# Theta and the token products take their token tiles in the order in which the MLP finishes them

## The chip, the cores and the metric

The kernel runs on one core of a Trainium2 chip. The metric is the device time of one execution in microseconds; the time of a kernel is the median of several runs. The engines are TensorE (PE, matmuls; PEld is its weight load), VectorE (DVE), ScalarE (ACT), GpSimd (POOL) and SyncE (SP), which issues most of the DMAs. Each engine works through its own instructions in one fixed order and waits for the others by semaphores.

## What is computed

The program is a chain of three blocks on 2 batches of 768 tokens: bucketed attention (8 heads of 64), a block that adds the real part of a 2D Fourier transform and then an MLP (512 to 2048 to 512), and a last block. The change lies in the last block:

```python
def _moe2_ref(x, w_theta, w_tok_r, w_tok_i, w_ch):
    theta = x @ w_theta
    cos_t, sin_t = (np.cos(theta), np.sin(theta))
    zr = x * cos_t
    zi = x * sin_t
    yr = np.einsum('ts,bsd->btd', w_tok_r, zr)
    yi = np.einsum('ts,bsd->btd', w_tok_i, zi)
    y = yr + yi
    u = x + y
    return (u + np.maximum(u @ w_ch, 0.0)).astype(np.float32)
```

Its x is the MLP block's result. The token products (yr, yi) sum over all 768 source tokens s, so the order in which the source tiles are added is free.

## The kernel before, in words

Tokens are held in 6 tiles of 128 (NT = 6). Most products are made of three matmuls (P3): high by high, high by low, low by high, where each operand is split into a rounded high part and a rest.

**The MLP** (`mlp1`, `mlp2`, from line 799 for the second) works on groups of two tiles. Group g holds tiles g and g + 3, so the groups finish tiles 0 and 3, then 1 and 4, then 2 and 5. This is also the list `order` of line 716, [0, 3, 1, 4, 2, 5], which the layer norm uses. At the end of each group two DVE operations add the sums, which lie in two PSUM banks, to the residual u of the two tiles.

**theta** (line 821) then goes tile by tile over u. For each tile PE transposes it in four pieces (`psf<-ident,u` in the trace); ACT rounds the transposed tile to xh, DVE makes the rest xl; ACT makes a copy xs, which SP writes to DRAM (`xT<-xs`); PE makes 12 products with the theta weights (`psf<-wthh,xh` and the like). Then come the argument reduction, sine and cosine on ACT (nn<-psf first), POOL and DVE (rr<-nn,psf first), and the four parts of z (zr and zi, high and low) for the tile. The buffers xh, xl and xs exist once, nn and rr twice.

**tok_sum** (line 862) makes one half (384 of the 768 target tokens) of the token product of one batch: for each of 4 blocks kd of 128 channels, 6 source tiles of 6 matmuls, 144 in all. With `s_outer` the source tiles are the outer loop and four banks are summed at once, so that the sum can follow theta. Otherwise each block kd is summed on its own. **conv_tok** (line 1025) converts the token weights of a half, two pieces for each source tile (real and imaginary, n = 2s + r), in the order n = 0 to 11: a DMA brings them (`r<-in_wtok`), two ACT operations and one DVE operation decode them, ACT writes the high part (w1h; wtx for source tile 5) and POOL the low part. The second half's pieces are written over those of the first half.

**The order of the work.** Outside attention nothing is ordered by hand: a planner places the instructions of each engine by their data dependences and by priorities that `at` and `timed` give (a start and a step in us), on a timeline of its own. Around the change the program's order is: theta of batch 0, the MLP of batch 1 (groups 0, 1, and `mlp1` of group 2), the first half's token weights, `mlp2` of group 2 (line 1034), theta of batch 1 (line 1055), tok_sum of batch 0, half 0 (line 1058), tok_sum of batch 1, half 0, with `s_outer` (line 1068), the second half's weights (line 1070), the channel product of batch 0 half 0, then the second halves. Sums named psm in the trace use three PSUM banks (the MLP and most token sums); those named psf use five (theta, and the sum with `s_outer`).

Most instructions are issued through one helper, so the line in the trace is L62 for nearly all of them; the names of the tiles tell them apart.

Of the kernel before, what the change touches and what calls it, by code (L numbers as in the profile page):

```python
# [22 lines left out]
NT = S // 128  # L23
# [10 lines left out]
def f(t):  # L34
    return t.bitcast(F32)
# [35 lines left out]
def fused_kernel(ctx, tc, A, out):  # L71
# [9 lines left out]
    def mm(o, l, r, st, sp):  # L81
        PE.matmul(o, l, r, start=st, stop=sp)
# [4 lines left out]
    def stt(eng, out, in0, in1, op, scale=1.0):  # L87
        if eng is V:
            return V.scalar_tensor_tensor(out=out, in0=in0, scalar=scale, in1=in1, op0=ALU.mult, op1=op)
        assert scale == 1.0  # L90
        return eng.tensor_tensor(out=out, in0=in0, in1=in1, op=op)
# [34 lines left out]
    def PS1():  # L126
        return PS(now[0])
# [588 lines left out]
    order = [g + 3 * i for g in range(3) for i in range(2)]  # L716
# [101 lines left out]
    z_t = {}  # L818
    xTd = {b: mk(dr_p, [128, 4, S], F32, f"xT{b}") for b in range(B)}

    def theta(b, wth, zt):
        x2 = u_t[b]
        for t in range(NT):
            c = slice(128 * t, 128 * t + 128)
            pt = PS1()
            for kd in range(4):
                PE.transpose(pt[:, 128 * kd:128 * kd + 128], x2[:, t, 128 * kd:128 * kd + 128], ident)
            xh = zt([128, 4, 128], F32R, "xh")
            xl = zt([128, 4, 128], F32R, "xl")
            pk = pt.rearrange("p (k n) -> p k n", k=4)  # L830
            AC.activation(out=xh, in_=pk, func=AF.Copy)
            V.tensor_tensor(out=xl, in0=pk, in1=f(xh), op=ALU.subtract)
            xs = zt([128, 4, 128], F32, "xs")
            AC.activation(out=xs, in_=pt.rearrange("p (k n) -> p k n", k=4), func=AF.Copy)
            SY.dma_start(out=xTd[b][:, :, c], in_=xs)
            xx = (xh, xl)
            th = PS1()
            n = 0
            for kd in range(4):
                for a, k in P3:  # L840
                    mm(th, xx[a][:, kd], wth[k][:, kd], n == 0, n == 11)
                    n += 1
            nn = zt([128, DM], F32, "nn")
            AC.activation(out=nn, in_=th, func=AF.Identity, scale=1.0 / TWO_PI, bias=c_mag)
            PL.tensor_scalar(out=nn, in0=nn, scalar1=1.0, scalar2=-MAGIC, op0=ALU.mult, op1=ALU.add)
            rr = zt([128, DM], F32, "rr")
            V.scalar_tensor_tensor(out=rr, in0=nn, scalar=-PC1, in1=th, op0=ALU.mult, op1=ALU.add)
            V.scalar_tensor_tensor(out=rr, in0=nn, scalar=-PC2, in1=rr, op0=ALU.mult, op1=ALU.add)
            PL.tensor_scalar(out=rr, in0=rr, scalar1=3.1415925, scalar2=-3.1415925, op0=ALU.min, op1=ALU.max)
            V.tensor_scalar(out=nn.bitcast(U32), in0=rr.bitcast(U32), scalar1=0x7FFFFFFF, scalar2=None, op0=ALU.bitwise_and)  # L850
            AC.activation(out=rr, in_=rr, func=AF.Sin)
            AC.activation(out=nn, in_=nn, func=AF.Sin, scale=-1.0, bias=c_pi2)
            for r, trig in enumerate((nn, rr)):
                stt(V if r else PL, trig, trig, x2[:, t], ALU.mult)
                zh, zl = z_t[b][r]
                AC.activation(out=zh[:, t], in_=trig, func=AF.Copy)
                stt(PL if r else V, zl[:, t], trig, f(zh[:, t]), ALU.subtract)
            yield

    TH = 384  # L860

    def tok_sum(b, half, wt, kx, s_outer=False):

        c = slice(TH * half, TH * half + TH)
        xt, uh, ul = kx
        SY.dma_start(out=xt, in_=xTd[b][:, :, c])

        def sums(ps, kd, s):
            n = 0
            for r in range(2):  # L870
                for a, k in P3:
                    mm(ps[:, 0:TH], z_t[b][r][a][:, s, 128 * kd:128 * kd + 128], wt(k, r, s), s == 0 and n == 0, s == NT - 1 and n == 5)
                    n += 1

        def split(ps, kd):
            V.tensor_tensor(out=xt[:, kd], in0=ps[:, 0:TH], in1=xt[:, kd], op=ALU.add)
            AC.activation(out=uh[:, kd], in_=xt[:, kd], func=AF.Copy)
            V.tensor_tensor(out=ul[:, kd], in0=xt[:, kd], in1=f(uh[:, kd]), op=ALU.subtract)

        if s_outer:  # L880
            pss = [PS1() for _ in range(4)]
            for s in range(NT):
                for kd in range(4):
                    sums(pss[kd], kd, s)
                yield
            for kd in range(4):
                split(pss[kd], kd)
            return
        for kd in range(4):
            ps = PS1()  # L890
            for s in range(NT):
                sums(ps, kd, s)
            split(ps, kd)
            yield
# [109 lines left out]
    def zt(shape, dt, tag):  # L1004
        n = turn.get(tag, 0)
        turn[tag] = n + 1
        return mk(zts[n % len(zts) if tag in ("nn", "rr") else 0], shape, dt, tag)
# [3 lines left out]
    zz = lambda p, tag: mk(p, [128, NT, DM], F32R, tag)  # L1011
    z_t[0] = [[zz(x_p, "x"), zz(zb_p, "za")], [zz(zb_p, "zb"), zz(zb_p, "zc")]]
    timed(theta(0, wth, zt), T["z0"], 2)
    now[0] = "m"
    mlp(1, T["m1"], range(2))
# [5 lines left out]
    def wt(k, r, s):  # L1021
        n = 2 * s + r
        return w1z[k][:, TH * n:TH * n + TH] if n < 10 else wtx[0][:, 2 * k + n - 10]
# [29 lines left out]
    timed(conv_tok(0, 10), t0 - 14, 1)  # L1053
    now[0] = "f"
    timed(theta(1, wth, zt), t0 - T["tp"], 1)
    now[0] = "m"
    k0 = operands(xt_p, xt_p)
    timed(tok_sum(0, 0, wt, k0), t0 + 20, 2)
    zt2_p.release()
    zt_p.release()  # L1060
# [5 lines left out]
    k1 = operands(xt1_p, u1_p)  # L1066
    now[0] = "f"
    timed(tok_sum(1, 0, wt, k1, True), t0 + 40, 2)
    now[0] = "m"
    timed(conv_tok(1), t0 + 40, 1)  # L1070
    timed(tok_out(0, 0, wch, k0), t0 + 56, 1)
    k0 = operands(xt_p, xt_p)
    timed(tok_sum(1, 1, wt, k0), t0 + 60, 2)
    now[0] = "f"
    timed(tok_out(1, 0, wch, k1), t0 + 70, 1)
# [109 lines left out]
```

## Time and profile before

| | us |
|---|---|
| median of 3 runs | 728.55 |
| the runs | 728.55, 734.02, 728.23 |
| the profiled execution | 728.28 |
| its span, first to last instruction | 726.5 |
| PE busy in the span | 664.8 |
| DVE, ACT, POOL busy | 402.6, 372.7, 370.1 |

All rows below are from the one profiled execution, with times from the span's start. A share of busy time is an average over stages with different limits; the stages around theta and the token sums are read by themselves.

### The profile page before, as it was taken

The page shows a single profiled execution, that of the slowest core. Times are in us where ns is not written, and L with a number is a line of the kernel's source. Part 1 is how long each engine was busy: PE and PEld are TensorE (multiplying, and loading weights), DVE is VectorE, ACT ScalarE, POOL GpSimd, SP SyncE. Part 2 cuts the span into 40 slices and gives each one's busy share as a digit, 9 for nine tenths or more (in the row PEclk, how much of TensorE's full clock was granted, in tenths as well). Part 3 has the DMA queues.
Part 4 walks back from the last instruction along what each step waited for, and adds up shares of the span by engine and source line. Part 5 has one row for each costly group of instructions (what it writes and reads, how often), then busy time and mean ns, then how long its engine had stood idle before and what let it go on. Part 6 is the DMA issues. An engine that isn't in the chain of part 4 may idle for free.

```text
span 726.5 us, 13450 instructions
## 1 busy us (share of the span) xinstructions
PE 664.8 (92%) x5424; PEld 510.9 (70%) x5424; DVE 402.6 (55%) x655; ACT 372.7 (51%) x597; POOL 370.1 (51%) x312
## 2 busy tenths in 40 slices
PE   5798988669668898999999999999999899999998
PEld 2365556557557655786686786687485599999997
DVE  1566787865999665543377583255422476751222
ACT  2565565766988898773423152065325676730010
POOL 3787789586878888776660020033403446930000
PEclk9999999978699999999999999999999999999999
DMA  9896967459889999776560043011004631720202
GB/s 327 186 187 141 157 121 142 93 164 213 197 206 240 269 231 253 151 145 124 102 195 27 13 120 65 1 45 30 1 1 145 223 89 39 234 81 25 88 1 87
DMA packets 161469, 93.68 MB, mean 129 GB/s; under 512 B 137088, under 2 KB 147584, under 8 KB 161408
## 3 DMA queue, kind: packets, MB, share of 16 engines
q1 hardware_dynamic: 159472, 86.27, 51.3%
q0 software_dynamic: 1936, 6.57, 2.6%
q8 instruction: 42, 0.69, 0.4%
q14 instruction: 19, 0.16, 0.1%
HBM read 49.82 MB, written 6.29 MB: 77 GB/s over the span
## 4 chain that ended last, share of the span: by engine, by line
PE 48%; POOL 10%; issue 9%; DMA 6%; ACT 5%; DVE 4%; POOLq 0%; SPq 0%; DVEq 0%; ACTq 0%
PE psm L62 31%; PE psf L62 14%; POOL p L62 3%; ACT r L62 2%; PE pso L62 2%; POOL w1l L62 2%; DMA x<-p 2%; POOL stk L62 2%; PE pss L62 1%; DMA r<-in_wtok 1%; DMA r<-in_w 1%; POOL pt L62 1%; DVE r L62 1%; ACT stk L62 1%; POOL w2l L62 1%
## 5 line engine op out<-in xcount | busy, mean ns | idle before, releaser
L62 PE MATMUL psm<-unT,w1h 128*128 128x256 f16 x768 | 130.4, 274 | 0.1
L62 PE MATMUL psm<-unT,w1l 128*128 128x256 f16 x384 | 105.2, 274 | 0.0
L62 DVE SCALAR_TENSOR_TENSOR r<-r 128x512 uint32<-128x512 uint32 (+1 forms) x64 | 64.6, 1016 | 51.9 <-ACT r L62 49.2
L62 PEld LDWEIGHTS <-w1h 128*128 128x128 f16 (+1 forms) x774 | 75.1, 99 | 15.5 <-issue 4.5
L62 PEld LDWEIGHTS <-hh 128*128 128x128 f16 x384 | 37.1, 98 | 42.8 <-issue 2.2
L62 POOL TENSOR_TENSOR w1l<-r,w1h 128x384 fp32r<-128x384 f32 (+1 forms) x36 | 41.9, 1178 | 43.5 <-ACT w1h L62 43.5
L62 PE MATMUL pss<-stk 128*128 128x384 f32 x192 | 48.8, 384 | 15.2 <-ACT p L62 9.4
L64 PE MATMUL pss<-stk 64*128 64x384 f32 (+1 forms) x288 | 55.4, 470 | 6.4 <-ACT p L64 3.2
L62 DVE TENSOR_REDUCE nm<-pss 128x1 f32<-128x768 f32 x48 | 44.9, 949 | 29.0 <-PE pss L62 28.8
L62 PE MATMUL psm<-w2h,hl 128*128 128x512 f16 x192 | 60.3, 379 | 0.0
L62 PE MATMUL psm<-w2l,hh 128*128 128x512 f16 x192 | 59.8, 379 | 0.2 <-POOL w2l L62 0.2
L62 ACT ACTIVATE r<-r,chalf 128x512 uint32<-128x512 uint32 (+1 forms) x64 | 46.1, 720 | 26.2 <-DMA r<-in_wtok 10.2
L62 PE MATMUL psm<-w2h,hh 128*128 128x512 f16 x192 | 59.3, 379 | 0.0
L62 POOL TENSOR_TENSOR p<-p,p 128x768 f16<-128x768 f32 x32 | 54.7, 1715 | 6.6 <-ACT p L62 5.5
L62 ACT ACTIVATE p<-pss,nm 128x768 f32<-128x768 f32 x48 | 42.5, 892 | 28.1 <-DVE nm L62 23.3
L62 DVE SCALAR_TENSOR_TENSOR hl<-psm,hh 128x512 f16<-128x512 f32 x48 | 32.8, 687 | 41.9 <-ACT hh L62 41.8
L64 DVE TENSOR_REDUCE nm<-pss 128x1 f32<-128x768 f32 x48 | 43.6, 950 | 19.9 <-PE pss L64 19.8
L62 ACT ACTIVATE hh<-psm 128x512 f16<-128x512 f32 x48 | 28.2, 590 | 40.4 <-PE psm L62 40.4
L62 PEld LDWEIGHTS pss<-stk 128*128 128x128 f32 x192 | 34.6, 204 | 20.2 <-ACT p L62 11.9
L62 PEld LDWEIGHTS <-w1l 128*128 128x128 f16 x384 | 37.7, 98 | 5.7 <-issue 1.2
L62 ACT ACTIVATE r<-r 128x512 f32<-128x512 f32 (+1 forms) x64 | 39.5, 618 | 0.0
L62 POOL TENSOR_TENSOR stk<-tt,stk 64x768 fp32r<-64x768 f32 x16 | 31.1, 1945 | 11.5 <-issue 9.6
(322 smaller groups left out, 1552.2 us busy)
## 6 DMA issues: line engine op xcount, KB each, us to landing
r<-in_w SPq DMA_DIRECT2D x32, 512.0 KB, 4.5
r<-in_wtok SPq DMA_DIRECT2D x24, 384.0 KB, 3.8
vr<-in_v SPq DMA_DIRECT2D x8, 390.0 KB, 3.6
stk<-stk SPq DMA_DIRECT2D x16, 192.0 KB, 3.8
xT<-xs SPq DMA_DIRECT2D x12, 256.0 KB, 2.6
xt<-xT SPq DMA_DIRECT2D x4, 768.0 KB, 5.8
ct<-in_ct POOLq DMA_DIRECT2D x4, 579.0 KB, 7.3
sn<-in_sn POOLq DMA_DIRECT2D x4, 576.0 KB, 8.2
```

Source lines behind the costliest of these rows:

```text
L62: return fn(*a, **k)
L64: self.last = fn(*a, **k)
```

## The change

Theta and both forms of the token sum take the tiles in `order` instead of 0 to 5; the closing matmul of a sum is that of the last tile in `order`, which is tile 5 in both.

```diff
     def theta(b, wth, zt):
         x2 = u_t[b]
-        for t in range(NT):
+        for t in order:
             c = slice(128 * t, 128 * t + 128)
...
-                    mm(ps[:, 0:TH], z_t[b][r][a][:, s, 128 * kd:128 * kd + 128], wt(k, r, s), s == 0 and n == 0, s == NT - 1 and n == 5)
+                    mm(ps[:, 0:TH], z_t[b][r][a][:, s, 128 * kd:128 * kd + 128], wt(k, r, s), s == 0 and n == 0, s == order[-1] and n == 5)
...
         if s_outer:
             pss = [PS1() for _ in range(4)]
-            for s in range(NT):
+            for s in order:
                 for kd in range(4):
                     sums(pss[kd], kd, s)
...
             ps = PS1()
-            for s in range(NT):
+            for s in order:
                 sums(ps, kd, s)
```

Both batches use these functions. The order in which `conv_tok` makes the weights stays 0 to 5.

## Rows read from the trace of the kernel before

**Rows 1.** The page, part 1: busy us, share of span, instructions.
```profile
PE 664.8 (92%) x5424; PEld 510.9 (70%) x5424; DVE 402.6 (55%) x655; ACT 372.7 (51%) x597; POOL 370.1 (51%) x312
```

**Rows 2.** Busy time by stage: stretch, length, then engines, PEclk, DMA share, GB/s.
```profile
573.85:580.65 6.80, 4.58 (x28) 4.25 (x26) 2.92 (x6) 5.21 (x10) 2.87 (x3) 1.00 0.96 314
...
614.24:639.38 25.14, 25.14 (x146) 25.14 (x146) 18.28 (x19) 20.57 (x41) 23.62 (x19) 1.00 0.61 189
...
sum 242.96, PE 240.72 PEld 207.38 DVE 104.14 ACT 96.98 POOL 75.44; mean PE 40.12 PEld 34.56 DVE 17.36 ACT 16.16 POOL 12.57
```

**Rows 3.** Waits of PE, 480 to 727: us in total, times, longest.
```profile
PE psf L62 <- DVE u L62: 2.2, 1, 2.2
```

**Rows 4.** PE's timeline, 578 to 582: start, us, operation, idle before it.
```profile
578.09 0.34 PE L62 MATMUL psm<-w1l,x 128*128 128x384 f32 x1
580.65 0.66 PE L62 MATMUL psf<-ident,u 128*128 128x128 f32 x4 [2.22 <-DVE u L62]
581.06 0.42 PE L62 MATMUL psm<-w1h,za 128*128 128x384 f32 x1
...
581.84 0.34 PE L62 MATMUL psm<-w1h,x 128*128 128x384 f32 x1
```

**Rows 5.** DVE's timeline, 568 to 582.
```profile
568.82 0.69 DVE L62 TENSOR_TENSOR xl<-psf,xh 128x512 fp32r<-128x512 f32 x1 [0.43 <-ACT xh L62]
...
579.30 0.69 DVE L62 SCALAR_TENSOR_TENSOR rr<-nn,psf 128x512 f32<-128x512 f32 x1 [0.58 <-POOL nn L62]
579.91 1.28 DVE L62 SCALAR_TENSOR_TENSOR u<-psm,u 128x512 f32<-128x512 f32 x2
```

**Rows 6.** ACT's timeline, 568 to 630.
```profile
568.21 0.58 ACT L62 ACTIVATE xh<-psf 128x512 fp32r<-128x512 f32 x1
...
576.69 0.76 ACT L62 ACTIVATE r<-r,chalf 128x512 uint32<-128x512 uint32 x1 [1.37 <-DMA r<-in_wch]
...
577.89 0.67 ACT L62 ACTIVATE nn<-psf,cmag 128x512 f32<-128x512 f32 x1
...
629.20 0.98 ACT L62 ACTIVATE w1h<-r 128x384 fp32r<-128x384 f32 x2
```

**Rows 7.** DVE's timeline: the MLP's last additions, batch 0, and batch 1's second group.
```profile
359.25 1.29 DVE L62 SCALAR_TENSOR_TENSOR u<-psm,u 128x512 f32<-128x512 f32 x2
...
525.46 1.29 DVE L62 SCALAR_TENSOR_TENSOR u<-psm,u 128x512 f32<-128x512 f32 x2 [3.07 <-PE psm L62]
```

**Rows 8.** PE's timeline: theta's products of batch 1, second to fourth tile.
```profile
568.84 0.50 PE L62 MATMUL psf<-wthh,xh 128*128 128x512 f32 x1
...
571.95 0.60 PE L62 MATMUL psm<-w2h,hl 128*128 128x512 f16 x2
...
585.16 0.39 PE L62 MATMUL psf<-wthh,xh 128*128 128x512 f32 x1
...
592.96 0.39 PE L62 MATMUL psf<-wthh,xh 128*128 128x512 f32 x1
```

**Rows 9.** SP's timeline, 586 to 623: issues of DMAs.
```profile
586.71 21.90 SPq L62 DMA_DIRECT2D xT<-xs  x4
...
622.42 0.58 SPq L62 DMA_DIRECT2D xt<-xT  x1
```

**Rows 10.** POOL's timeline: low parts of the token weights, both halves.
```profile
570.76 1.03 POOL L62 TENSOR_TENSOR w1l<-r,w1h 128x384 fp32r<-128x384 f32 x1 [1.69 <-ACT w1h L62]
...
637.03 2.37 POOL L62 TENSOR_TENSOR w1l<-r,w1h 128x384 fp32r<-128x384 f32 x2 [0.41 <-ACT w1h L62]
641.36 2.52 POOL L62 TENSOR_TENSOR wtx<-r,wtx 128x384 fp32r<-128x384 f32 x2 [1.96 <-ACT wtx L62]
```

**Rows 11.** DVE's timeline: the last part of z, batch 1.
```profile
633.70 0.68 DVE L62 SCALAR_TENSOR_TENSOR za<-nn,u 128x512 fp32r<-128x512 f32 x1
```

**Rows 12.** PE's timeline: first products of z's last tile, first of the second half.
```profile
635.06 0.51 PE L62 MATMUL psf<-wtx,u 128*128 128x384 f32 x2
...
647.55 0.35 PE L62 MATMUL psm<-w1h,u 128*128 128x384 f32 x1
```

## The prediction

> **What bounds the kernel now.** I read the whole page first, then a table by stage, then the waits, then single instructions. The page has TensorE (PE) busy for 92% of the span and every other engine for near half [rows 1]. The table by stage then takes the second half: over six stretches from 480.00 us to the last matmul at 722.96, PE is busy for 240.72 of 242.96 us, and the loss of 2.2 us lies in one of them, 573.85 to 580.65, where it works 4.58 us of 6.80; the granted clock stays at 1.00 there [rows 2]. The list of PE's waits in that half has one entry: 2.2 us, once, for VectorE's (DVE) write of u [rows 3]. So behind 480 us the kernel is a queue of matmuls with one hole of 2.22 us, and no order of tiles can give back more than that hole there.
>
> PE's timeline shows what stands at the hole: token products of batch 0 run up to 578.09, and the next four of the same block (za, zb, zb, zc of the fifth token tile, from 581.06) are held, since ahead of them in PE's order stand the four transposes of theta's third tile of batch 1 (tile 2), which wait for u [rows 4]. Tile 2 is written with tile 5 by the two additions that end the third MLP group. DVE makes them only at 579.91: ahead in its queue is the theta reduction of the second tile (rr<-nn,psf), which waits for GpSimd (POOL) [rows 5]. POOL waits for ScalarE (ACT), whose rounding of that tile (nn<-psf) comes at 577.89, behind 1.37 us of waiting for a weight load (in_wch) and the decoding of what it brought [rows 6].
>
> **What the change removes.** In the new order theta's third and fourth tiles are 1 and 4. Both are written by the additions of the second MLP group at 525.46 [rows 7], some 45 us before they are wanted. Nothing then ties the third tile to the end of the third group. Tile 2 comes fifth; in before the fifth tile's transposes lie behind the fourth's first products at 592.96 [rows 8], over 11 us behind the additions. The wait goes, if PE has something else to run until 580.65, that is 6.80 us of work from 573.85 on. It has the 30 matmuls of the first block of token sums, at 25.14/144 = 0.175 us each [rows 2] 5.2 us; and the third tile's theta: four transposes, 0.41 us from 580.65 to the next matmul [rows 4], and 12 products, which for the second tile run from 568.84 to 571.95 with one MLP matmul among them [rows 8], about 2.9 us. Together 8.5 us against 6.8: enough by 1.7. Where a part of it runs before 573.85 it pushes the MLP's end back by as much, which costs PE nothing.
>
> **What it adds: no work.** The same instructions on other slices: six theta tiles for each batch, 144 matmuls for each token sum, the same DMAs and the same weights. For batch 0 all six tiles are there long before theta takes them (its MLP's last additions come at 359.25 [rows 7]): 0 us.
>
> **What it moves.** Three things, each costed at 0 with its cover:
> - Tile 2's copy to DRAM goes out fifth, not third, on SP's queue. The load of batch 1's first residual half needs tiles 0 to 2; in before it is issued at 622.42, behind all six copies [rows 9]. Cover: the sixth copy is out before it too.
> - The fifth token tile's weights are now wanted fourth. The last of them is converted at 571.79 [rows 10]; their sums start at about 577.9 (two of six run before the hole [rows 4]) and would start 6 x 0.175 = 1.05 us sooner. Cover: 5 us.
> - The second half's weights overwrite the first half's, in the order 0 to 5, while batch 1's sums now free these in the order 0, 3, 1, 4, 2, 5. The sums run 25.14 us [rows 2], 4.2 us a tile, so tile 1's place comes free 4.2 us later and tile 2's 8.4 us later, at 614.24 + 5 x 4.2 = 635.2; the weights of tiles 3 and 4 queue behind. Six low parts at 1.19 us on POOL from about 636 end at 643, the last two, 2.52 us together, at 645.7 [rows 10]. The first reader starts at 647.55 [rows 12], the last tile's 30 matmuls (5.2 us) later. Cover: 4 us for those wanted first, 7 for the last. If it were gone, each us late would be one of PE's, which has nothing else to run there.
>
> **What is late next.** With the hole closed, batch 1's sums start at 612.0 and want the last tile's z at 632.8. In before that z ends at 634.38 [rows 11], only 0.7 us ahead of its first matmul at 635.06 [rows 12]. But theta lost time at its third tile: these products start 16.3 us behind the second's (568.84, 585.16), the fourth's 7.8 us behind the third's [rows 8]. So theta should end some 8 us sooner, and this slack grows. Were theta to end where it did, 1.6 us of the gain would go (the bound above).
>
> **The sum.** The profiled execution took 728.28 us (span 726.5); less 2.22 it is 726.06. The median of the runs is 728.55, 0.27 above the profiled one, so the forecast is 726.3 us. What the trace can't show is the order in which the planner, with its own timeline, puts the new work on each engine. That is bounded by the rows: at best nothing beyond the 2.22, at worst the slower rivals below; I take 0, nearest to how theta's second tile fared, whose products came with no idle time.
>
> **The rivals.**
> (a) *The hole stays in another form.* The second block of token sums needs a PSUM bank, and the additions that write u also free the MLP's two banks: its first matmul starts at 581.84, right behind them [rows 4, 5]. If the third tile's operands aren't ready at 578.43, PE runs the four left-over matmuls (0.7 us) and waits for the same DVE operation: 728.55 - 0.7 = 727.9. For it: ACT is what was late in before. Against it: the third tile gives PE 3.3 us of other work. [...]
> (b) *Slower: theta jumps ahead on PE and waits for ACT.* The planner may now put the third tile's 12 products right behind the MLP. Their xh is ACT's work; if it stands where the second tile's nn stood, at 577.89, then xh (0.58) [rows 6] and xl (0.69) [rows 5] make the products start at about 579.2. PE would stand up to 579.2 - 573.85 = 5.35 us in place of 2.22: 731.7. It decides on how many token matmuls stand ahead of them: 30 hide it all, under 18 the kernel is slower than before. Against it: the second tile's products came 0.02 us behind the start of xl, with MLP matmuls in front and no idle.
> (c) *Slower: the second half's weights jam ACT.* If tile 2's conversion, held to 635.2 instead of its 629.20 [rows 6], stands in ACT's queue ahead of the last theta tile's work, that z comes 6 us late, at 640.4 against 632.8 wanted: 7.6 lost less 2.2, near 734. Against it: theta should be done with ACT by then.
>
> **How the numbers follow.** Forecast 0.60 (725.5 to 727.0: the full gap, give or take 0.7); (a) 0.22, with the case that the planner moves nothing and the time stays at 728.5; (b) 0.12; (c) 0.06. The range goes from 725.0 (the lowest run, 728.23, less the gap, less 1 for run and overlap) to 730.0, half of (b)'s price: it leaves out the worse half of (b) and (c), a little over a tenth. A measurement tells about 1% (7.3 us) from no change. The gain can't reach that by what stands above: faster 0.02. Slower by over 1% needs (c) with some of (b): 0.05. Within it: 0.93.
>
> **What would show it.** Right: no wait of PE for DVE's u behind 545 us and PE busy throughout behind the MLP's end; theta's third tile inside or right behind the third MLP group, its products under 10 us after the second's; tile 2's transposes fifth; batch 1's sums starting near 612. Wrong: a PE wait for xl or xh near 574 to 580 (b), for u with a token matmul at its head (a), for z or the second half's weights between 630 and 655 (c), or idle time of PE anywhere that was dense.

## The result, and the profile after

The changed kernel takes 735.11 us (median of 10 runs, 733.68 to 737.14). The kernel before, run beside it, took 730.5 us. The ratio is 1.0069, 95% interval [1.0046, 1.0091]: about 5 us slower, where 2.2 us less was forecast, and outside the range (725.0 to 730.0). The profiled execution took 733.68 us, with a span of 731.9.

One remark on the base. In later runs of the kernel before, the medians were 730.7 to 731.3 and single runs went from 726.9 to 735.8. So its profiled execution of 728.28 us is a low one of its spread. Ratios below are taken over the undisturbed runs and needn't equal the quotient of the medians over all runs; single profiles are used to see where time goes.

The page's first part and the list of PE's waits of the changed kernel (380 to 732 us: total, times, longest):

```profile
PE 664.9 (91%) x5424; PEld 509.9 (70%) x5424; DVE 403.7 (55%) x655; ACT 372.4 (51%) x597; POOL 371.2 (51%) x312
```
```profile
PE psm L62 <- DVE xt L62: 4.0, 1, 4.0
PE psf L62 <- ACT xh L62: 2.6, 2, 2.3
```

PE has the same 5424 matmuls and all but the same busy time [rows 1]. The one entry of before, for u [rows 3], is gone. In its place stand 2.6 us for ACT's xh and a new 4.0 us for DVE's xt.

**The front.** PE's timeline around the old hole (start, us, operation, idle before it and what ended it):

```profile
568.17 0.50 PE L62 MATMUL psf<-wthh,xh 128*128 128x512 f32 x1 [0.31 <-ACT xh L62]
...
568.74 0.27 PE L62 MATMUL psf<-ident,u 128*128 128x128 f32 x1
...
571.31 0.49 PE L62 MATMUL psf<-ident,u 128*128 128x128 f32 x3
...
573.14 0.59 PE L62 MATMUL psm<-w2h,hl 128*128 128x512 f16 x2
573.39 0.52 PE L62 MATMUL psm<-w1h,x 128*128 128x384 f32 x1
...
576.39 0.34 PE L62 MATMUL psm<-w1l,zb 128*128 128x384 f32 x1
579.03 0.50 PE L62 MATMUL psf<-wthh,xh 128*128 128x512 f32 x1 [2.30 <-ACT xh L62]
```

The third tile's four transposes (psf<-ident,u) run inside the MLP; its last two matmuls start at 573.14 and the token products of batch 0 follow, as forecast. But PE's order then has the third tile's products behind only 17 token matmuls (the first at 573.39, the last at 576.39), and these products wait 2.30 us. ACT's timeline says for what:

```profile
576.11 0.76 ACT L62 ACTIVATE r<-r,chalf 128x512 uint32<-128x512 uint32 x1 [1.35 <-DMA r<-in_wch]
...
577.31 0.68 ACT L62 ACTIVATE nn<-psf,cmag 128x512 f32<-128x512 f32 x1
...
578.40 0.59 ACT L62 ACTIVATE xh<-psf 128x512 fp32r<-128x512 f32 x1
```

It is the wait of before [rows 6]: ACT stands 1.35 us in front of a load of in_wch, the weights of the channel product, then decodes it, then does the second tile's nn and the third tile's xh. Before, this chain ran on over POOL and DVE to u; now it ends at xh. The hole is 2.30 us where it was 2.22.

**The back.** PE's timeline from the start of batch 1's sums to the second halves:

```profile
613.90 0.33 PE L62 MATMUL psf<-w1h,u 128*128 128x384 f32 x1
...
644.93 0.34 PE L62 MATMUL psm<-ks,wchl 128*128 128x384 f32 x1
649.24 0.74 PE L62 MATMUL psm<-ks,wchh 128*128 128x384 f32 x2 [3.96 <-DVE xt L62]
...
652.98 0.35 PE L62 MATMUL psm<-w1h,u 128*128 128x384 f32 x1
```

The stalled matmul belongs to the channel product of batch 0 half 0, which has four blocks of 12 matmuls and three PSUM banks. Its fourth block can start only when an eviction has freed the first block's bank. These evictions are DVE's `xt<-psm,xt`. DVE's and ACT's timelines:

```profile
644.75 0.56 DVE L62 SCALAR_TENSOR_TENSOR r<-r 128x384 uint32<-128x384 uint32 x1 [1.20 <-ACT r L62]
645.22 0.55 DVE L62 TENSOR_TENSOR u<-xt,u 128x384 fp32r<-128x384 f32 x1
645.69 0.55 DVE L62 TENSOR_TENSOR xt<-psf,xt 128x384 f32<-128x384 f32 x1
646.16 2.56 DVE L62 TENSOR_TENSOR u<-xt,u 128x384 fp32r<-128x384 f32 x2
648.64 1.47 DVE L62 SCALAR_TENSOR_TENSOR xt<-psm,xt 128x384 f32<-128x384 f32 x3
```
```profile
636.65 0.64 ACT L62 ACTIVATE r<-r,chalf 128x384 uint32<-128x384 uint32 x1 [3.62 <-DMA r<-in_wtok]
...
638.60 0.53 ACT L62 ACTIVATE w1h<-r 128x384 fp32r<-128x384 f32 x1
...
643.57 0.65 ACT L62 ACTIVATE r<-r,chalf 128x384 uint32<-128x384 uint32 x1 [1.71 <-DMA r<-in_wtok]
...
644.56 0.92 ACT L62 ACTIVATE u<-xt 128x384 fp32r<-128x384 f32 x2
```

Read from the bottom up. The evictions (648.64) stand behind the splits of batch 1's sum (u<-xt,u). The splits need ACT's copies u<-xt (644.56), which stand behind the decoding of a second-half weight; that stood 1.71 us waiting for its load. DVE's own decoding of that weight (644.75) is ahead of the splits as well. The two splits at 646.16 take 1.28 us each, where the one at 645.22 took 0.55; POOL makes low parts beside them (646.00 to 648.30), but that this slows them wasn't tested. In the kernel before two such splits took 2.22 us (642.07), so it is not new. The load is late for the reason that POOL and SP show:

```profile
639.21 1.04 POOL L62 TENSOR_TENSOR w1l<-r,w1h 128x384 fp32r<-128x384 f32 x1 [3.44 <-ACT w1h L62]
```
```profile
624.18 16.42 SPq L62 DMA_DIRECT2D r<-in_wtok  x6
...
640.28 0.33 SPq L62 DMA_DIRECT2D r<-in_wtok  x1
```

The raw weights land in a small ring of buffers r. A buffer comes free when POOL has made the low part from it, and POOL can write that only over a place that the sums have left. The sums now leave tile 2's place fifth, while its pieces still come third in the converting order; these hold their buffers, and the last load goes out at 640.28, just as POOL's low part of 639.21 ends (640.25). POOL had waited 3.44 us for ACT's high part of that piece (638.60). Tile 2's place was free at 634.70, where the sums' last tile begins, but ACT stood 3.62 us, until 636.65, in front of another late load: here one late load made the next one late. The rows don't name the piece; that it is tile 2's is argued from the order, and the first experiment tests it. In the kernel before the same six issues, and the first evictions, stood so (SP, then DVE):

```profile
624.31 9.41 SPq L62 DMA_DIRECT2D r<-in_wtok  x6
```
```profile
644.22 1.01 DVE L62 SCALAR_TENSOR_TENSOR xt<-psm,xt 128x384 f32<-128x384 f32 x2
```

There the last issue was over at 633.72, and the first eviction ended near 644.7, only 0.7 us before its bank was wanted (12 matmuls, 2.1 us, ahead of 647.55 [rows 12], so 645.4).

**The clock.** Busy time by stretch of the changed kernel (columns as [rows 2]):

```profile
645.00:649.20 4.20, 0.27 (x2) 0.00 (x0) 4.20 (x7) 1.80 (x5) 2.30 (x2) 1.00 0.00 0
649.24:651.00 1.76, 1.76 (x6) 1.76 (x7) 0.87 (x2) 0.00 (x0) 0.00 (x0) 0.60 0.22 81
651.00:653.00 2.00, 2.00 (x8) 2.00 (x8) 0.00 (x0) 0.00 (x0) 0.00 (x0) 0.50 0.34 125
653.00:660.00 7.00, 7.00 (x42) 7.00 (x41) 0.56 (x1) 0.00 (x0) 0.00 (x0) 1.00 0.43 149
```

Behind the gap PEclk, TensorE's granted clock, is 0.60 in the mean and then 0.50, until about 653; from there it is 1.00. The 12 matmuls of the fourth block take 3.74 us (649.24 to 652.98); at 0.175 each it would be 2.10, so 1.64 us more.

**The account.** From the last two matmuls of batch 1's MLP to the kernel's last matmul, the kernel before needs 149.35 us (573.26 to 722.61) and the changed one 154.91 (573.14 to 728.05): 5.56 more. The parts: 0.08 (2.30 for 2.22), 3.96 for the bank and 1.64 at the lower clock, together 5.68. Against this, the changed kernel ran four transposes ahead of this stretch that the kernel before has in it, 0.41 us [rows 4]; for equal work the difference is 5.97, of which 0.3 us has no row here. This stretch is called the tail below; each tail is that of one execution.

### The profile page after: what moved, and what is told of

Read it like the earlier page. It is cut to its first block, busy times and chain, and to the rows that moved or that the text cites. A ratio compares the mean times of both kernels' runs of the same rounds, so it can differ in the third digit from the quotient of the medians.

```text
span 731.9 us, 13444 instructions
## 1 busy us (share of the span) xinstructions
PE 664.9 (91%) x5424; PEld 509.9 (70%) x5424; DVE 403.7 (55%) x655; ACT 372.4 (51%) x597; POOL 371.2 (51%) x312
## 4 chain that ended last, share of the span: by engine, by line
PE 41%; POOL 12%; issue 10%; DMA 8%; ACT 7%; DVE 4%; SPq 0%; POOLq 0%; ACTq 0%; DVEq 0%
PE psm L62 28%; PE psf L62 10%; POOL p L62 3%; ACT r L62 3%; DMA r<-in_wtok 2%; POOL w1l L62 2%; DMA x<-p 2%; PE pso L62 2%; POOL stk L62 2%; POOL pt L62 1%; ACT p L62 1%; DMA r<-in_w 1%; ACT stk L62 1%; PE pss L62 1%; POOL w2l L62 1%
## 5 line engine op out<-in xcount | busy, mean ns | idle before, releaser
L62 DVE SCALAR_TENSOR_TENSOR r<-r 128x512 uint32<-128x512 uint32 (+1 forms) x64 | 62.8, 984 | 60.3 <-ACT r L62 55.6
```

The costliest lines, as they stand in the source:

```text
L62: return fn(*a, **k)
```

## The experiments

Theory: two queues, each with its own cause. In front, ACT's stand before the in_wch load, whatever tile comes next. At the back, the order in which the sums free the second half's weights no longer fits the order in which these are converted; the late load reaches PE over ACT's and DVE's queues and the bank. Rivals: the back comes from theta's new order; all of it comes from one cause, the wait for the in_wch load; the late load matters by itself, not what queues behind it. Each kernel was timed in five rounds beside the kernel before.

**The weights in the sums' order, added to the change.**

```diff
-        for n in range(n0, n1):
+        for n in ([2 * s + r for s in order for r in range(2)] if half else range(n0, n1)):
```

> The changed kernel, with the second half's token weights converted in the order 0, 3, 1, 4, 2, 5, in which batch 1's sums free their places. Theory A (the mismatch between the order of freeing and the order of converting makes the last loads late, ACT and DVE then hold their queues for them, and the evictions of the channel product stand behind): PE's 3.96 us wait for xt at 645 us goes, and with it the 12 matmuls at half clock behind it (1.7 us); the wait for xh near 577 us (2.3 us) stays. Span 731.9 - 5.6 = 726.3, time about 728. Rival B (the jam at 645 us comes from theta's other timing on DVE and POOL, whatever the order of the weights): the gap stays over 3 us and the time stays at 733 to 736.

Measured: 732.09 us, where about 728 was expected, ratio 1.0025 [0.9997, 1.0053]; tail 150.96. The interval still touches that of the changed kernel, so it is the waits that show the mend. PE's waits behind 500 us, and SP's six loads:

```profile
PE psf L62 <- ACT xh L62: 2.4, 2, 1.9
PE psm L62 <- DVE xt L62: 0.5, 1, 0.5
```
```profile
626.57 9.98 SPq L62 DMA_DIRECT2D r<-in_wtok  x6
```

The loads take 9.98 us in place of 16.42 and the wait for xt falls from 4.0 to 0.5, with theta and the sums still in the new order. The front stays. Not expected was the wait for xt that was left, nor that the clock now fell to 0.50 behind the front's gap of 1.91 us, where it had stayed at 1.00 behind 2.30 us in the changed kernel (the rows stand in the last section).

**Each half of the change by itself:** theta in the new order with the sums 0 to 5, then the sums in the new order with theta 0 to 5.

```diff
         x2 = u_t[b]
-        for t in range(NT):
+        for t in order:
```
```diff
-            for s in range(NT):
+            for s in order:
```

The second is made in both forms of the sum, with the closing matmul of the change.

> The kernel before with theta alone in the new order; the sums and the weights run 0 to 5. Theory A: places are freed in the order of converting, so no wait for xt near 645 us; the front's wait for xh near 577 us (2.3 us) as in the changed kernel; time about 728. Rival B: theta's timing makes the jam, so the wait of about 4 us near 645 us is there and the time is 733 to 736.

> The kernel before with the token sums alone in the new order; theta runs 0 to 5. Theory A: the hole of 2.2 us on u near 578 us stays, and near 645 us PE waits some 3 to 5 us for xt and then runs some matmuls at half clock: 728.3 + 5.6 = about 734. Rival B: no wait near 645 us, time as before, 727 to 731.

Measured: theta alone 731.93 us, ratio 1.0003 [0.9977, 1.0029], tail 151.33; sums alone 734.2 us, ratio 1.0054 [1.0021, 1.0088], tail 153.46. Waits of PE, theta alone and then sums alone:

```profile
PE psf L62 <- ACT xh L62: 2.5, 1, 2.5
PE psm L62 <- DVE xt L62: 0.9, 1, 0.9
PE psf L62 <- DVE za L62: 0.6, 1, 0.6
```
```profile
PE psf L62 <- ACT xh L62: 2.4, 2, 1.7
PE psf L62 <- DVE u L62: 2.2, 1, 2.2
PE psm L62 <- DVE xt L62: 1.9, 1, 1.9
```

Theta's order alone moves the hole from u to xh. PE also waits 0.9 us for xt, where none was expected, and 0.6 us for za, but the time can't be told from that of the kernel before. The sums' order alone keeps the hole on u and brings the late loads: SP's six take 15.99 us (10.00 with theta alone). So the jam of the loads is the sums', not theta's.

The late evictions aren't the sums' alone. From the channel product's first matmul, which ends batch 1's sums, to DVE's first eviction it is 5.00 us in the kernel before (639.22 to 644.22), 6.67 with theta alone (640.35 to 647.02), 7.74 with the sums alone (642.13 to 649.87) and 9.78 with both (638.86 to 648.64). How theta's order delays them, with its loads on time, wasn't tested. For the sums alone the time came as expected, but in part by luck: xt cost 1.9 us, less than the 3 to 5 expected and without the fall of the clock (PEclk 1.00 behind it), while two further waits for xh came (0.76 and 1.68), which no theory had.

**The in_wch weights converted later.** Here the decoding of in_wch is issued behind theta's last rounding (nn), so that ACT doesn't stand before it; after_gate has what it encloses issued behind the named instruction. It was added to the first experiment's kernel, to the kernel before, and to the changed kernel.

```diff
-            AC.activation(out=nn, in_=th, func=AF.Identity, scale=1.0 / TWO_PI, bias=c_mag)
+            gate["th"] = AC.activation(out=nn, in_=th, func=AF.Identity, scale=1.0 / TWO_PI, bias=c_mag)
...
-    timed(conv32(A["wch"], 4 * DM, flat3(wch[0]), flat3(wch[1])), t0 + 22, 1)
+    with after_gate("th"):
+        timed(conv32(A["wch"], 4 * DM, flat3(wch[0]), flat3(wch[1])), t0 + 22, 1)
```

> e1 with the conversion of the channel weights (in_wch) held until theta's last rounding on ACT, so that no decode of theirs stands in ACT's queue during theta. Theory F (the third tile's xh is late because ACT waits for an in_wch load ahead of it): the 2.3 us wait for xh near 577 us falls under 0.5, PE loses under 1 us behind 545 us, time about 725.5. Rival G (ACT is late from theta's own chain or the token weights): the wait stays over 1.5 us, time 728. Rival H: the conversions, now in a bunch behind theta, jam POOL or DVE before the channel product, with a new wait of PE between 630 and 650 us: 729 or more.

> The kernel before with the channel weights' conversion (in_wch) held until theta's last rounding on ACT; no tile order is changed. Theory F (both the old hole on u and the new wait on xh come from ACT standing in front of an in_wch load near 575 us): the hole of 2.2 us on u falls to 0.7 or less, the span by about 1.5 to 725. Rival (the old hole comes from the tile order): it stays at 1.5 us or more and the time is as before.

> The changed kernel with in_wch held as in e5, the second half's weights in the order 0 to 5. If front and back are two causes that add: the wait for xh near 577 us goes (under 0.8 in all), the wait for xt near 645 us stays at 3 us or more with slow matmuls behind it in some executions; time between after and e5, 731 to 734. If the back's jam is a consequence of the front's, it shrinks under 1.5 us.

Measured, in this order: 728.28 us, ratio 0.9963 [0.994, 0.9987], tail 147.67; 728.02 us, ratio 0.9946 [0.9918, 0.9973], tail 147.90; 734.23 us, ratio 1.0019 [0.9996, 1.0043], tail 152.81. The first missed its 725.5: PE still waits 0.7 us for xh and 1.0 us for xt, where under 1 us in all was expected. The second came as expected (span 724.9), and so did the third's waits, its time just above the 731 to 734. The waits of the kernel before with this edit alone, its nn on ACT and its additions on DVE:

```profile
PE psm L62 <- DVE xt L62: 0.4, 2, 0.2
PE psf L62 <- ACT xh L62: 0.4, 1, 0.4
```
```profile
573.24 0.67 ACT L62 ACTIVATE nn<-psf,cmag 128x512 f32<-128x512 f32 x1
```
```profile
575.92 1.28 DVE L62 SCALAR_TENSOR_TENSOR u<-psm,u 128x512 f32<-128x512 f32 x2
```

With tiles still in order 0 to 5, nn comes 4.65 us earlier than at 577.89 [rows 6], the additions 3.99 us earlier than at 579.91 [rows 5], and the hole on u is gone. So the hole can be closed without touching the order of the tiles; its cause was ACT's stand for in_wch. In the changed kernel the same edit removes the xh wait and leaves the back as it was:

```profile
PE psm L62 <- DVE xt L62: 4.2, 1, 4.2
```

So neither cause explains the other.

**The splits behind the evictions.** The splits of batch 1's first sum are issued behind the third eviction of the channel product. Added to the in-order kernel with late in_wch, and to the changed kernel, where the late load stays.

```diff
-            V.scalar_tensor_tensor(out=xt[:, m], in0=ps[:, 0:TH], scalar=0.0, in1=xt[:, m], op0=ALU.max, op1=ALU.add)
+            ev = V.scalar_tensor_tensor(out=xt[:, m], in0=ps[:, 0:TH], scalar=0.0, in1=xt[:, m], op0=ALU.max, op1=ALU.add)
+            if m == 2:
+                gate.setdefault("ev", ev)
...
-    timed(tok_sum(1, 0, wt, k1, True), t0 + 40, 2)
+    first = tok_sum(1, 0, wt, k1, True)
+    timed(take(first, NT), t0 + 40, 2)
...
+    with after_gate("ev"):
+        run(first)
```

> e5 with the splitting of batch 1's sums (12 operations on DVE and ACT) issued behind the channel product's third eviction. Theory A's last link (the evictions of the channel product, which free PSUM banks, stand behind these splits on DVE): the wait of 1.0 us for xt near 644 us goes, span 725.6 - 1.0 = 724.6, time about 727.3 at e5's median of 728.28. Rival: PE waits there for something else, or the splits are then late for the next channel product near 670 us: no gain.

> The changed kernel with the same splits behind the third eviction, the weights' order left at 0 to 5. Theory A: the late decode of the last weight piece still stands ahead of the evictions on DVE (its end was 645.3 us), the splits no longer: the wait for xt falls from 4.0 to 0.5 to 1.2 us and no matmuls at half clock follow; the wait of 2.3 us for xh stays; time 735.1 less 3 to 5. Rival (the late weights themselves hold PE): the wait stays over 3 us, or moves to w1h, w1l or wtx.

Measured: the first 726.82 us (6 runs), ratio 0.9924 [0.9901, 0.9947], tail 146.38, the wait for xt gone as expected, and only 0.4 us of xh waiting left; the second 732.75 us, ratio 1.0018 [0.9995, 1.0041], tail 150.00. The second's time lies a little above the expected 730 to 732, its interval just below that of the changed kernel. The second's waits and its DVE:

```profile
PE psf L62 <- ACT xh L62: 2.2, 1, 2.2
PE psm L62 <- DVE xt L62: 0.8, 1, 0.8
```
```profile
651.00 0.56 DVE L62 SCALAR_TENSOR_TENSOR r<-r 128x384 uint32<-128x384 uint32 x1 [3.96 <-ACT r L62]
651.48 1.48 DVE L62 SCALAR_TENSOR_TENSOR xt<-psm,xt 128x384 f32<-128x384 f32 x3
```

DVE still stands 3.96 us for the decoding of the late weight, and PE loses 0.8 us for xt in place of 4.0; no fall of the clock follows (PEclk 1.00 in the mean of 640 to 665). What hurt was the work queued between the late weight and the evictions. The rival that the load matters by itself falls, for all but these 0.8 us.

**Both edits on the old order.** Late in_wch and late splits, by the two diffs above, on the kernel before, tiles 0 to 5.

> The kernel before (tiles 0 to 5 everywhere) with both holds: in_wch behind theta's last rounding, the splits of batch 1's sums behind the channel product's third eviction. If the tile order itself is worth nothing once the queues are clear, PE loses under 0.6 us behind 545 us and the ratio to before is that of e11, 0.992 within 0.003. If the order gives the third tile's theta a head start that still counts, e11 stays ahead: this one 0.995 or more, with a wait of over 0.7 us on u or a token weight.

Measured: 727.39 us, ratio 0.9954 [0.9927, 0.998], tail 146.88; PE waits for nothing behind 500 us. Two stretches (columns as [rows 2]):

```profile
546.00:600.00 54.00, 54.00 (x277) 39.77 (x275) 25.34 (x42) 33.57 (x65) 25.58 (x26) 1.00 0.52 159
600.00:640.00 40.00, 40.00 (x228) 39.43 (x227) 26.82 (x30) 30.72 (x58) 28.70 (x24) 1.00 0.39 126
```

PE is busy in all of 546 to 640. Beside the new order with the same edits (146.38, intervals overlapping) no worth of the order can be told: with the four transposes that its tail lacks, 0.41 us, the two tails differ by 0.1. The ratio lies just outside the first expectation (0.992 within 0.003) and by its number in the second, but the wait that the second wanted isn't there. Both are faster than the kernel before and the changed one; the new order with all three edits has the lowest ratio.

| kernel | ratio | tail, us |
|---|---|---|
| before | 1 | 149.35 |
| the change | 1.0069 | 154.91 |
| change, weights in order | 1.0025 | 150.96 |
| theta alone | 1.0003 | 151.33 |
| sums alone | 1.0054 | 153.46 |
| change, splits late | 1.0018 | 150.00 |
| change, in_wch late | 1.0019 | 152.81 |
| change, weights in order, in_wch late | 0.9963 | 147.67 |
| the same, splits late | 0.9924 | 146.38 |
| before, in_wch late | 0.9946 | 147.90 |
| before, in_wch and splits late | 0.9954 | 146.88 |

The tails of all kernels with theta in the new order lack the four transposes (0.41 us).

## Why the prediction was wrong

**What bounds the kernel** was right, and so was the bound on the gain: one hole of 2.22 us, behind ACT's stand for in_wch. The two kernels with 0 and 0.4 us of waits left have tails 2.5 and 3.0 us under 149.35, the second 2.6 for equal work: 0.3 to 0.4 over the hole.

**"The wait goes, if PE has something else to run": failed.** The wait for u went, as it said, and PE had 8.5 us of other work. But the sum took all of this as usable, whatever its order and readiness. The planner put the products behind only 17 of the 30 token matmuls, and their xh was on ACT behind the same load. That is rival (b): its start of the products, about 579.2, was measured as 579.03, and its point of no gain, 18 matmuls, fits the 17 ahead and a hole longer by 0.08 us. The start is in part luck: (b) put xh at 577.89 and had the products wait for xl as well; measured, ACT ran 0.58 us earlier than before, xh stood behind nn and one more operation (578.40), and the first product didn't wait for xl. Its price of 731.7 was for products right behind the MLP, which didn't come. The cause of the hole had been read correctly up to in_wch, and then only the last link was costed.

**"What it moves", third point: failed, and it made the result.** The freeing order was seen and its delays were worked out, with a cover of 4 to 7 us. The cover was reckoned only to the first PE matmul that reads these weights (647.55), and for that reader it held: PE waits for no weight. Three things between were left out: the weights' raw buffers come free late too, so that loads go out late (640.28); ACT and DVE stand before a late load with other work behind them; and among this work are the evictions that free PE's next bank, with 0.7 us of slack in before. Measured: 3.96 us and 1.64 us of slower matmuls, where 0 was taken; part of the late evictions goes with theta's order, by a way that stays open. The price "each us late would be one of PE's" was also short by the clock.

**Rival (c)** had the right operations, the second half's weights in ACT's queue, but the wrong victim: the last tile's z. DVE's last za starts at 623.8, far ahead of batch 1's last sums, and PE doesn't wait for it. Its sum of 734 is near the measured time by accident.

**"What is late next"**: theta did end sooner, by 6.1 us (its last product at 606.12, 612.26 before), so the slack ahead of the last z grew as forecast; but batch 1's sums start at 613.90, near 614.24 [rows 2] and not at 612.0, since the hole in front stayed. **Rival (a)** didn't come: nothing at the front waits for a PSUM bank. Tile 2's late copy and the weights wanted sooner, the first two points of "what it moves", cost no PE wait, as forecast.

## What to carry to other kernels

When the order of readers changes, change the order of the writers that fill the places they leave, and follow a late writer not only to its reader but to everything behind it on each in-order engine, with the PSUM bank that the nearest eviction frees. A gap that ends in a wait for X should be traced to the first instruction that stood still, and that should be mended: moving one filler conversion closed a hole of 2.22 us on u that reordering the tiles only renamed (2.30 us for xh).

## What was not expected of the hardware

Whether TensorE's clock fell behind a gap wasn't told by the gap's length alone in these runs. PEclk in the 2 us after a gap: the changed kernel after 2.30 us, the first experiment after 1.91 us and theta alone after 2.49 us.

```profile
579.03:581.03 2.00, 2.00 (x10) 1.63 (x11) 2.00 (x4) 1.46 (x3) 1.29 (x1) 1.00 0.61 230
```
```profile
580.93:582.93 2.00, 2.00 (x7) 1.70 (x8) 2.00 (x4) 1.46 (x3) 1.28 (x1) 0.50 0.67 240
```
```profile
579.61:581.61 2.00, 2.00 (x10) 1.63 (x11) 2.00 (x4) 1.46 (x3) 1.29 (x1) 1.00 0.57 215
```

The shortest of the three is the one after which the clock was at 0.50; with the sums alone, a gap of 1.93 us left it at 1.00 (650.46 to 652.46). Both gaps of about 4 us were followed by a fall: to 0.60 and then 0.50 behind the 3.96 us at the back of the changed kernel (the rows under "The clock"), to 0.50 (649.57 to 651.57) behind 4.24 us in it with late in_wch. What sets off the fall isn't shown; the rows say only that near-equal gaps didn't end alike. In these executions the gap of 2.30 us cost no more than itself (PEclk 1.00 behind it), and that of 1.91 us cost 1.46 us on top: the 12 products behind it, with the four transposes among them, take 3.44 us in the changed kernel (579.03 to 582.47) and 4.90 us in the first experiment (580.93 to 585.83). Whether this is part of why the runs of one kernel spread was not tried.
